# Filler matmuls, later loads and one pair's transpose moved to TensorE in a fused attention and bilinear-FFN kernel

## The chip, the cores and the metric

The kernel runs on one core of one Trainium2 chip. The metric is the device time of one execution, in microseconds: 420.25 as the median of five runs, from 419.61 to 420.96. TensorE (PE in the profile) multiplies matrices, VectorE (DVE) and ScalarE (ACT) work element by element, GpSimd (POOL) issues the loads here, and SyncE (SP) issues DMA transposes.

## The reference

```python
# q, k, v: (8, 8, 576, 64) float32; bias_table: (32, 8)
scores = scale * np.matmul(q, k.transpose(0, 1, 3, 2))
bias = bias_table[bucket]                    # bucket from |i - j|
scores = scores + bias.transpose(2, 0, 1)[None, :, :, :]
attn = softmax(scores)                       # written out with max, exp and sum
attn_out = np.matmul(attn, v)
# x: (4608, 512), the heads of a token side by side
a = x @ w_a                                  # (512, 1536)
b = x @ w_b
out = (a * b) @ w_out                        # (1536, 512)
```

There are 8 batches with 8 heads of 576 tokens. The bias depends on the distance of two tokens alone and enters as a factor after the exponential.

## The kernel before

**Tiling.** Two heads make a pair, so there are 32 pairs, four to a batch; pair p belongs to batch p // 4. Of the 576 tokens the first 512 are four tiles of 128, and the last 64 are a tail. For each pair TensorE makes the scores by key tile (`qk`, line 407, and `qk_tail`), ScalarE takes the exponential (`ex`, 429), VectorE multiplies with the bias factor (`mul`, 434; the table lies in `W_sb`, loaded by `load_w`), and TensorE multiplies with v (`av_mm`, 561 and 565, with one more column of ones that gives the sum of the weights). `av_norm` (579, 580) divides by the sum on VectorE and writes the pair's result into `XG[p % 2]`, token by token. `t_x` turns it into the layout that the FFN needs, `xn_sb`, with one tile for each of the four pairs of a batch.

**Two ways to transpose.** For pairs 4 to 30 `t_x` issues two DMA transposes from SP's queue (588 for the four main tiles, 591 for the tail). For the first four pairs and the last one it uses TensorE: `tr_x` (602) transposes tiles into a half of the PSUM tile `trb`, and `copy_x` (299 on VectorE, 297 on ScalarE) copies them into `xn_sb`. The queries and keys of batches 0 and 1 are transposed on TensorE as well, those of later batches by DMA, half a batch at a time (`t_half`, 379 and 371).

**FFN.** It runs over nine chunks of 512 tokens. A chunk has 36 units of four matmuls: `ff_in` (626) makes pa and pb from `xn_sb`, all four pairs of a batch in one sum, ScalarE copies pa (`ff_ha`, 633), VectorE multiplies (`ff_g`, 636), and `ff_o_mm` (663) multiplies with w_out; `ff_o_out` (668) copies to `ob` and ScalarE's queue stores it. Chunk c takes the main tokens of batch c; chunk 8 takes all tails.

**Order.** It is written by hand; each engine does its instructions in the order of the program text. The first pairs follow the string `opening`, whose tokens are steps: `<name` is a load on POOL's queue, `S` scores, `E` exponential, `M` product, `AV` and `N` attention matmul and its normalisation, `X` and `CX` transpose and copy of the result, `TQ`, `TK`, `TZ` and `CQ`, `CK`, `CZ` the same for queries, keys and tails, `F`, `H`, `G` parts of the FFN, and `w` a matmul of zeros into a tile `warm` that nothing reads. From pair 7 on a loop over slots s (one pair each) lays out the steps of pair s and the attention matmuls of pair s - 1, with nine FFN units in between (`U`). At the end of a slot stand the transposes and loads for later batches. `load_half(b, g)` loads half g of batch b: keys, queries, with g = 0 the tails too, and values. The b of the loop counts from 0, so b = 3 is the fourth batch.

```python
late = [A(3, 4), lambda: t_x(s - 1), U]
...
if s % 4 == 1 and 2 <= b < B:
    load_vt(b)
if s % 4 == 3:
    load_half(b + 1, 0)
if s % 4 == 1 and b > 2:
    load_half(b, 1)
```

`load_vt(b)` loads the tails of v of a batch (170) into one of two buffers; it waits until the attention matmuls of batch b - 2 have read it. POOL's loads stand in one queue, so what comes behind waits as well.

Of the kernel before, what the change touches and what calls it, by code (L numbers as in the profile page):

```python
# [13 lines left out]
def kernel(  # L14
# [11 lines left out]
    nc = tc.nc  # L26
    FP32 = mybir.dt.float32
# [4 lines left out]
    B, H, S, Dh = 8, 8, 576, 64  # L32
# [183 lines left out]
                            op=mybir.AluOpType.subtract)  # L216
    warm = ps_av.tile([128, 512], FP32, tag="av", name="warm")

    def warm_up(n):
        for _ in range(n):  # L220
            nc.tensor.matmul(out=warm[:, :], lhsT=zero_sb[:, 0:128], rhs=zero_sb[:, :],
                             start=True, stop=True)

    warm_up(5)
    nc.scalar.activation(out=eb_sb[0:NB, :], in_=bt_sb[0:NB, :], func=ACTF.Exp)
# [358 lines left out]
    def t_x(p, jqs=range(5), eng=None):  # L584
        b, hp = divmod(p, 4)
        c0 = SM * B + ST * b
        if 4 <= p < NP - 1:
            nc.sync.dma_start_transpose(
                out=xn_sb[hp][:, SM * b:SM * b + SM].rearrange("d (j c) -> d j c", j=4),
                in_=XG[p % 2][:, 0:4, :, :].rearrange("p j h d -> p (j h d)"))  # L590
            nc.sync.dma_start_transpose(
                out=xn_sb[hp][:, c0:c0 + ST],
                in_=XG[p % 2][0:ST, 4, :, :].rearrange("p h d -> p (h d)"))
            return
        tr_x(p, jqs)
        copy_x(p, jqs, eng)

    def tr_x(p, jqs):
        st[p]["tx", jqs[0]] = ps = tr_half()
# [5 lines left out]
    def copy_x(p, jqs, eng):  # L605
        b, hp = divmod(p, 4)
        c0 = SM * B + ST * b
        ps = st[p]["tx", jqs[0]]
        q0, q1 = 128 * jqs[0], min(SM, 128 * jqs[-1] + 128)
        copy(eng, xn_sb[hp][:, SM * b + q0:SM * b + q1], ps[:, 0:q1 - q0])  # L610
        if jqs[-1] == 4:
            copy(eng, xn_sb[hp][:, c0:c0 + ST], ps[:, SM - q0:S - q0])
# [98 lines left out]
    def v_next(s):  # L711
# [8 lines left out]

    opening = """
        <k0 <q0 <q123h0 <tk <k23 <k1 <W0 <v0 <vtb <Wtb <W1 <W3 <vta <W2 <tq <R1 <q123h1 <v1 <R0 <Wta
        <wa0 <wb0 TK0 PD0 CK0:A PD1 w TQ0 PU1 CQ00:D CQ01:D w S000 PU0 TQ20 E000 PC1 TQ10 S001 CQ20:D
        CQ10:D TQ30 E001 PC0 TZ1 CQ30:D S011 CZ1:A PC2 <vt1b <uq <vt1a <R2 <wa1 <q4 <R3 <k4 <wb1 <vb1b
        <q5 <k5 <uk <vb1a <wb2 <q6 <q7 <k6 <k7 <wa2 <wo S010 PF0 TK3 PF1 E011 TK2 CK3:D CK2:D E010 w
        S300 M001 TK1 E300 M000 KS CK1:D EK w S101 V0:D E101 w S100 E100 M101 w S200 AV00 M300 E200 S301
        N00 TZ0 E301 M100 X00 S201 CX00:D AV10 E201 M200 N10 CZ0:A M201 X10 TQ11 M301 CX10:A T0 CQ11:A
        V1:D TQ31 ET0 S111 M010 AV20 E111 MT0 T1 N20 AV30 CQ31:A ET1 M011 TQ21 LH S110 N30 X20 CQ21:A
        S310 CX20:A MT1 X30 E110 AV01 CX30:D M111 FA0a E310 M110 S210 FB0a N01 HA0a S211 E210 FA1a G0a
        AV11 HA1a M210 E211 X01 T2 N11 TZ0x CX01:A T3 ET2 FB1a M211 X11 FA2a G1a CX11:A S311 MT2 HA2a  # L730
# [11 lines left out]

    def step(token):
        nonlocal nxt
        if token == "w":
            warm_up(1)
            return
        if token[0] == "<":
            load(token[1:])
            return  # L750
        name, _, e = token.partition(":")
        eng = ACT if e == "A" else nc.vector
        kind = name.rstrip("0123456789abfx")
        num = name[len(kind):]
        if kind in ("FA", "HA", "FB", "G"):
            unit = (0, int(num[:-1]), 256 if num[-1] == "b" else 0, 512 if num[-1] == "f" else 256)
            if kind in ("FA", "FB"):
                ff_in(*((wa_sb, "pa") if kind == "FA" else (wb_sb, "pb")), *unit)
                nxt += 1
            else:  # L760
                (ff_ha if kind == "HA" else ff_g)(*unit)
            return
        if kind == "FO":
            ff_o_mm(0, int(num[0]), int(num[1]))
            nxt += 1
            return
        if kind == "HO":
            ff_o_out(0, int(num))
            return
        i = [int(x) for x in num.rstrip("x")]  # L770
        p = i[0] if i else 0
        first = p < 4
        jqs = None
        if len(i) > 1 and i[1] < 2:
            jqs = ((h0, h1) if first else ((0, 1, 2), (3, 4)))[i[1]]
        second = int(num.endswith("x"))
        if kind == "TQ":
            tr_qh(p, i[1]) if len(i) > 1 else tr_q(p)
        elif kind == "CQ":
            copy_qh(p, i[1], eng) if len(i) > 1 else copy_q(p, eng)  # L780
        elif kind == "TK":
            tr_k(p)
        elif kind == "CK":
            copy_k(p, eng)
        elif kind == "TZ":
            tr_tails(second, p)
        elif kind == "CZ":
            copy_tails(second, p, eng)
        elif kind == "KS":
            tail_keys0()  # L790
        elif kind == "EK":
            ex_keys0()
        elif kind == "S":
            qk_half(p, i[1], (i[2],)) if first else qk(p, 0, (i[1],))
        elif kind == "E":
            ex_half(p, i[1], i[2]) if first else ex(p, i[1])
        elif kind == "M":
            mul_half(p, i[1], i[2]) if first else mul(p, i[1])
        elif kind == "T":
            qk_tail(p)  # L800
        elif kind == "ET":
            ex_tail(p)
        elif kind == "MT":
            mul_tail(p)
        elif kind == "V":
            b, g = divmod(p, 2)
            v_in(b, 4 * g, 4 * g + 4, eng)
        elif kind == "AV":
            av_mm(p, jqs, *((ps_ff, "ffn") if first and i[1] == 0 and p % 2 else ()))
        elif kind == "N":  # L810
            av_norm(p, jqs)
            if not first and i[1] == 1:
                t_x(p)
        elif kind == "X":
            tr_x(p, jqs)
        elif kind == "CX":
            copy_x(p, jqs, eng)
        elif kind == "PU":
            pad_z(1, p)
        elif kind == "PF":  # L820
            nc.vector.memset(tl[0][64 * p:64 * p + 64, :, :, Dh - Dh * p:128 - Dh * p], 0.0)
        elif kind == "PC":
            if p == 2:
                pad_ones(1)
            else:
                nc.vector.memset(vt[1][64 * p:64 * p + 64, :, 1 - p, :], 0.0)
        elif kind == "PD":
            pad_x(p)
        elif kind == "LH":
            load_half(2, 0)  # L830
            load_half(2, 1)
        elif kind == "LV":
            load_vt(2)
        else:
            raise ValueError(token)
# [4 lines left out]
    t_half(2, 0)  # L840

    quotas = {7: 9, 8: 9}
    for s in range(7, NP + 1):
        new = s < NP
        U = "unit"
        A = lambda *jq: (lambda: av(s - 1, jq))
        steps = []
        if new:
            steps += [lambda: (qk(s, 0), ex(s, 0))]
        if new:  # L850
            head = [U, lambda: ex(s, 1), A(0, 1, 2), U, lambda: mul(s, 0), lambda: t_q(s + 1), U,
                    lambda: mul(s, 1)]
            late = [A(3, 4), lambda: t_x(s - 1), U]
            if shared(s):
                pair = [lambda: v_next(s), lambda: (qk(s, 2), ex(s, 2), ex_rows(s)), U,
                        lambda: ex(s, 3), U, lambda: mul(s, 2), lambda: mul_rows(s)]
            else:
                pair = [lambda: v_next(s), lambda: (qk(s, 2), ex(s, 2)), U, lambda: ex(s, 3),
                        lambda: t_k(s + 1, ACT), U, lambda: mul(s, 2)]
            tail = [lambda: (qk_tail(s), ex_tail(s)), U, U, lambda: mul_tail(s)]  # L860
            if s % 4 == 0:
                steps += head + late + [U] + pair + [lambda: mul(s, 3)] + tail
            else:
                steps += head + pair + late + [U, lambda: mul(s, 3)] + tail
        else:
            ff["late"] = True
            steps += [A(0, 1, 2), U, U, U, A(3, 4), lambda: t_x(s - 1, (0, 1, 2)), U, U, U,
                      lambda: t_x(s - 1, (3, 4)), U, U, U]
        b = s // 4 + 1
        if s % 4 == 2 and b < B:  # L870
            t_half(b, 0)
        if s % 4 == 0 and 2 <= b - 1 < B:
            t_half(b - 1, 1)
        if s % 4 == 1 and 2 <= b < B:
            load_vt(b)
        if s % 4 == 3:
            load_half(b + 1, 0)
        if s % 4 == 1 and b > 2:
            load_half(b, 1)
        quota = quotas.get(s, 9)  # L880
        seen, put = 0, 0
        nu = sum(1 for x in steps if x is U)
        for x in steps:
            if x is U:
                seen += 1
                n = (quota * seen + nu - 1) // nu - put
                put_units(n)
                put += n
            else:
                x()  # L890
# [31 lines left out]
```

## Time and profile before

| | us |
|---|---|
| median of five runs | 420.25 (419.61 to 420.96) |
| the profiled execution | 420.24 |
| its span | 418.5 |
| TensorE matmul busy | 405.6 |
| ScalarE busy | 250.5 |
| VectorE busy | 237.3 |
| GpSimd busy | 134.0 |
| granted TensorE clock | 1.00 |

The span is from the first to the last recorded instruction of one execution; the run's time has some more around it. Rows of the timeline give the start, the length of the group, the engine and line, the operation with output and inputs, the count, and in brackets how long the engine had stood still and what ended that. Rows of the waits give the sum, the count and the longest. Matmul rows overlap: the time from start to start is shorter than the length of one.

### The profile page before, as it was taken

The numbers are of one execution on the slowest core, as the hardware profiler recorded it, in microseconds if no ns is written. First come the engines' busy times: TensorE is split into PE (matmuls) and PEld (weight loads), VectorE is DVE, ScalarE is ACT, GpSimd is POOL, SyncE is SP. The second block draws the span as 40 slices with busy tenths as digits, with TensorE's granted clock in tenths as the row PEclk, the third lists the DMA queues.
The fourth block names the chain that finished last, engine by engine and source line by source line (L and its number), as shares of the span: only waits on it lengthen the run. The fifth ranks groups of instructions, "written<-read, shape, count | busy, mean of one in ns | idle before, by whom it ended". The sixth has DMA issues, their size and how long they took to land.

```text
span 418.5 us, 9152 instructions
## 1 busy us (share of the span) xinstructions
PE 405.6 (97%) x3643; PEld 212.0 (51%) x3643; DVE 237.3 (57%) x566; ACT 250.5 (60%) x388; POOL 134.0 (32%) x191
## 2 busy tenths in 40 slices
PE   8879999989999999999999999999999999999996
PEld 3457674535555544555555555455545555444443
DVE  5778987446654776467645675476547661330430
ACT  3978885466766765667657673866567742322321
POOL 6947629669108700690049201600000000000000
PEclk9999999999999999999999999999999999999999
DMA  8999999999939980999179905940420012002004
GB/s 102 168 195 187 204 148 144 146 210 130 125 59 163 135 101 20 164 149 116 22 136 156 137 16 117 145 91 17 91 89 16 16 39 77 1 2 101 2 0 100
DMA packets 136427, 42.22 MB, mean 101 GB/s; under 512 B 114328, under 2 KB 131608, under 8 KB 136384
## 3 DMA queue, kind: packets, MB, share of 16 engines
q0 software_dynamic: 81712, 20.27, 56.2%
q1 hardware_dynamic: 49232, 12.02, 20.1%
q10 hardware_dynamic: 5440, 9.34, 7.2%
q8 instruction: 28, 0.46, 0.5%
q14 instruction: 15, 0.12, 0.1%
HBM read 39.18 MB, written 9.45 MB: 116 GB/s over the span
## 4 chain that ended last, share of the span: by engine, by line
PE 77%; DMA 13%; POOL 6%; issue 1%; ACTq 0%; SPq 0%; ACT 0%; DVE 0%; POOLq 0%
PE pb L626 20%; PE pa L626 20%; PE po L663 19%; PE av L565 7%; PE qk L407 6%; DMA wo<-in_moe_w_out_dram 4%; DMA wb<-in_moe_w_b_dram 3%; DMA kn<-in_k_dram 2%; DMA xn<-XG 2%; DMA vn<-in_v_dram 2%; PE av L561 2%; PE qkt L478 1%; POOL W L236 1%; DMA bias_tab<-tab_sb 1%; POOL qn L132 1%
## 5 line engine op out<-in xcount | busy, mean ns | idle before, releaser
L429 ACT ACTIVATE at<-qk 128x1024 bf16<-128x1024 f32 x112 | 113.4, 1029 | 28.6 <-PE qk L407 10.7
L636 DVE TENSOR_TENSOR g<-pb,ha 128x512 bf16<-128x512 f32 (+1 forms) x116 | 76.0, 655 | 75.4 <-PE pb L626 58.7
L626 PE MATMUL pa<-xn,wa 128*128 128x512 bf16 (+1 forms) x464 | 112.7, 365 | 1.3 <-DMA xn<-XG 1.3
L626 PE MATMUL pb<-xn,wb 128*128 128x512 bf16 (+1 forms) x464 | 112.5, 365 | 0.6 <-DMA wb<-in_moe_w_b_dram 0.6
L633 ACT ACTIVATE ha<-pa 128x512 f32<-128x512 f32 (+1 forms) x116 | 66.6, 574 | 66.1 <-PE pa L626 66.0
L663 PE MATMUL po<-wo,g 128*128 128x512 bf16 x420 | 98.7, 379 | 0.0
L434 DVE TENSOR_TENSOR at<-at,W 128x1024 bf16<-128x1024 bf16 x112 | 74.9, 685 | 21.1 <-ACT at L429 21.1
L626 PEld LDWEIGHTS <-wa 128*128 128x128 bf16 x464 | 41.6, 98 | 45.5 <-issue 6.3
L626 PEld LDWEIGHTS <-wb 128*128 128x128 bf16 x464 | 40.9, 98 | 42.0 <-issue 4.7
L663 PEld LDWEIGHTS <-g 128*128 128x128 bf16 x420 | 38.3, 98 | 43.0 <-issue 2.5
L579 DVE RECIPROCAL rc<-av 128x6 f32<-128x6 f32 (+3 forms) x96 | 16.3, 170 | 52.4 <-PE av L565 52.2
L668 ACT ACTIVATE ob<-po 128x512 f32<-128x512 f32 x35 | 21.0, 600 | 40.0 <-PE po L663 31.9
L565 PE MATMUL av<-vm,at 128*128 128x65 bf16 x896 | 41.2, 194 | 0.0
L170 POOL DMA_DIRECT2D vt<-in_v_dram x12 | 7.9, 670 | 103.1 <-PE av L565 99.8
L565 PEld LDWEIGHTS <-at 128*128 128x128 bf16 x896 | 37.2, 98 | 6.2
L132 POOL DMA_DIRECT2D qn<-in_q_dram x48 | 36.4, 808 | 12.0 <-DMA wo<-in_moe_w_out_dram 7.9
L580 DVE TENSOR_TENSOR XG<-av,rc 128x384 bf16<-128x384 f32 (+3 forms) x96 | 36.2, 377 | 3.3
L141 POOL DMA_DIRECT2D kn<-in_k_dram x48 | 36.2, 794 | 2.8 <-PE trb L362 1.4
L561 PE MATMUL av<-vt,att 128*128 128x130 bf16 x152 | 33.3, 219 | 0.0
L407 PE MATMUL qk<-QB,KB 64*128 64x512 bf16 x192 | 29.2, 381 | 0.4 <-ACT at L429 0.3
L508 ACT ACTIVATE att<-qkt 128x576 bf16<-128x576 f32 x24 | 15.5, 648 | 13.1 <-PE qkt L480 13.1
L561 PEld LDWEIGHTS <-att 128*128 128x128 bf16 x152 | 15.0, 98 | 7.7 <-issue 1.6
(102 smaller groups left out, 314.7 us busy)
## 6 DMA issues: line engine op xcount, KB each, us to landing
out_dram<-ob ACTq DMA_DIRECT2D x32, 256.0 KB, 2.8
vn<-in_v_dram POOLq DMA_DIRECT2D x16, 256.0 KB, 6.5
kn<-in_k_dram POOLq DMA_DIRECT2D x48, 64.0 KB, 5.1
qn<-in_q_dram POOLq DMA_DIRECT2D x48, 64.0 KB, 4.5
wa<-in_moe_w_a_dram POOLq DMA_DIRECT2D x3, 512.0 KB, 9.3
wb<-in_moe_w_b_dram POOLq DMA_DIRECT2D x3, 512.0 KB, 9.6
wo<-in_moe_w_out_dram POOLq DMA_DIRECT2D x1, 1536.0 KB, 16.6
xn<-XG SPq DMA_TRANSPOSE x54, 3.3
```

The lines of the kernel that those rows point to most:

```text
L132: nc.gpsimd.dma_start(out=by_tile(qn[b % 2])[:, h0 // 4, t, :, :], in_=q[b, h0:h1, 128 * t:128 * t + 128, :].transpose([1, 0, 2]))
L141: nc.gpsimd.dma_start(out=by_tile(kn[b % 2])[:, h0 // 4, t, :, :], in_=k[b, h0:h1, t:SM:NM, :].transpose([1, 0, 2]))
L407: nc.tensor.matmul(out=ps[:, hh, :], lhsT=kT[r, t, :], rhs=qT[r, :, :], start=True, stop=True)
L429: nc.scalar.activation(out=at[:, :, :], in_=ps[:, :, :], func=ACTF.Exp, scale=scale)
L434: nc.vector.tensor_tensor(out=at[:, :, :], in0=at[:, :, :], in1=w[:, :, S - 1 + t:S - 1 + t - SM:-1], op=MULT)
L561: nc.tensor.matmul(out=pav[:, slot, :, :], lhsT=weights_tail(p, jq), rhs=vt[i][:, hp, :, :], start=True, stop=True)
L565: nc.tensor.matmul(out=pav[:, slot, hh, :], lhsT=weights(p, t, hh, jq), rhs=vm[i][:, 2 * hp + hh, t, :], start=False, stop=True, skip_grou ...
L580: nc.vector.tensor_tensor(out=xg[0:np_, j0:j0 + n, :, :], in0=pav[0:np_, s0:s0 + n, :, 0:Dh], in1=r.unsqueeze(3).to_broadcast([np_, n, 2, ...
L626: nc.tensor.matmul(out=ps[:, 0:n], lhsT=w[df // 4][:, mc, 128 * (df % 4):128 * (df % 4) + 128], rhs=xn_sb[mc][:, 512 * c + lo:512 * c + lo ...
L633: nc.scalar.activation(out=ha[:, 0:n], in_=ff["pa", df, lo][:, 0:n], func=ACTF.Copy)
L636: nc.vector.tensor_tensor(out=g_sb[df][:, lo:lo + n], in0=ff["pb", df, lo][:, 0:n], in1=ff["ha", df, lo][:, 0:n], op=MULT)
L663: nc.tensor.matmul(out=po[:, :], lhsT=g_sb[df][:, 128 * tt:128 * tt + 128], rhs=wo_sb[:, df, :], start=(df == 0), stop=(df == NDF - 1))
```

## The change

- Fillers: `w` now has a count, and `wa` writes to a tile of its own in the pool of the attention results. In the opening the two single `w` ahead of the scores of pair 0 become `w1` and `w4`, `w2` is added behind those scores, and `wa4` behind `AV10`. The other `w` stay at one.
- Loads: the first half of the batch with b = 3 is loaded in slot 9 instead of 7 and its second half in slot 10 instead of 9; the first half of b = 4 in slot 12 instead of 11. The later ones stay in their slots.
- Pair 7, the last pair of batch 1, is transposed by `tr_x` and `copy_x`, three query tiles and then two, in the place where the two DMA transposes were issued.

```diff
-    def warm_up(n):
+    def warm_up(n, dst=None):
         for _ in range(n):
-            nc.tensor.matmul(out=warm[:, :], lhsT=zero_sb[:, 0:128], rhs=zero_sb[:, :],
-                             start=True, stop=True)
+            nc.tensor.matmul(out=(warm if dst is None else dst)[:, :], lhsT=zero_sb[:, 0:128],
+                             rhs=zero_sb[:, :], start=True, stop=True)
...
-        if 4 <= p < NP - 1:
+        if 4 <= p < NP - 1 and p != 7:
...
+    def t_pair(p):
+        for jqs in ((0, 1, 2), (3, 4)) if p == 7 else (range(5),):
+            t_x(p, jqs)
...
-        <wa0 <wb0 TK0 PD0 CK0:A PD1 w TQ0 PU1 CQ00:D CQ01:D w S000 PU0 TQ20 E000 PC1 TQ10 S001 CQ20:D
+        <wa0 <wb0 TK0 PD0 CK0:A PD1 w1 TQ0 PU1 CQ00:D CQ01:D w4 S000 w2 PU0 TQ20 E000 PC1 TQ10 S001 CQ20:D
...
-        N00 TZ0 E301 M100 X00 S201 CX00:D AV10 E201 M200 N10 CZ0:A M201 X10 TQ11 M301 CX10:A T0 CQ11:A
+        N00 TZ0 E301 M100 X00 S201 CX00:D AV10 wa4 E201 M200 N10 CZ0:A M201 X10 TQ11 M301 CX10:A T0 CQ11:A
...
-        if token == "w":
-            warm_up(1)
+        if token[0] == "w":
+            warm_up(int(token[-1]), ps_av.tile([128, 512], FP32, tag="av", name=f"fill{nxt}")
+                    if token[1] == "a" else None)
             return
...
+    load_slot = {bb: 9 if bb == 3 else 12 if bb == 4 else 4 * bb - 5 for bb in range(3, B)}
...
-            late = [A(3, 4), lambda: t_x(s - 1), U]
+            late = [A(3, 4), lambda: t_pair(s - 1), U]
...
-        if s % 4 == 3:
-            load_half(b + 1, 0)
-        if s % 4 == 1 and b > 2:
-            load_half(b, 1)
+        for bb in range(3, B):
+            for g in range(2):
+                if s == load_slot[bb] + (2 - (bb < 5)) * g:
+                    load_half(bb, g)
```

More of the change, by code (lines that the diff above doesn't have):

```diff
@@ L722 @@
         <k0 <q0 <q123h0 <tk <k23 <k1 <W0 <v0 <vtb <Wtb <W1 <W3 <vta <W2 <tq <R1 <q123h1 <v1 <R0 <Wta
-        <wa0 <wb0 TK0 PD0 CK0:A PD1 w TQ0 PU1 CQ00:D CQ01:D w S000 PU0 TQ20 E000 PC1 TQ10 S001 CQ20:D
+        <wa0 <wb0 TK0 PD0 CK0:A PD1 w1 TQ0 PU1 CQ00:D CQ01:D w4 S000 w2 PU0 TQ20 E000 PC1 TQ10 S001 CQ20:D
         CQ10:D TQ30 E001 PC0 TZ1 CQ30:D S011 CZ1:A PC2 <vt1b <uq <vt1a <R2 <wa1 <q4 <R3 <k4 <wb1 <vb1b
-        <q5 <k5 <uk <vb1a <wb2 <q6 <q7 <k6 <k7 <wa2 <wo S010 PF0 TK3 PF1 E011 TK2 CK3:D CK2:D E010 w
-        S300 M001 TK1 E300 M000 KS CK1:D EK w S101 V0:D E101 w S100 E100 M101 w S200 AV00 M300 E200 S301
-        N00 TZ0 E301 M100 X00 S201 CX00:D AV10 E201 M200 N10 CZ0:A M201 X10 TQ11 M301 CX10:A T0 CQ11:A
+        <q5 <k5 <uk <vb1a <wb2 <q6 <q7 <k6 <k7 <wa2 <wo S010 PF0 TK3 PF1 E011 TK2 CK3:D CK2:D E010 w1
+        S300 M001 TK1 E300 M000 KS CK1:D EK w1 S101 V0:D E101 w1 S100 E100 M101 w1 S200 AV00 M300 E200 S301
+        N00 TZ0 E301 M100 X00 S201 CX00:D AV10 wa4 E201 M200 N10 CZ0:A M201 X10 TQ11 M301 CX10:A T0 CQ11:A
         V1:D TQ31 ET0 S111 M010 AV20 E111 MT0 T1 N20 AV30 CQ31:A ET1 M011 TQ21 LH S110 N30 X20 CQ21:A
```

## The prediction

> **What bounds the kernel now.** I read the page first: the busy row by slices, and the DMA row under it. Each slice is 10.46 us.
>
> ```profile
> PE   8879999989999999999999999999999999999996
> DMA  8999999999939980999179905940420012002004
> ```
>
> TensorE is full from the fourth slice on except for one 8, the slice from 83.7 to 94.2 us. The loss that a change can recover is in the first three slices and in that one. DMA is full up to 115 us. Next the waits of TensorE, then the chain that ended last, in order of time.
>
> ```profile
> PE trb L602 <- DVE XG L580: 1.6, 3, 0.9
> PE pa L626 <- DMA xn<-XG: 1.3, 1, 1.3
> PE pb L626 <- DMA wb<-in_moe_w_b_dram: 0.6, 1, 0.6
> ```
> ```profile
> 72.47 8.44 DMA kn<-in_k_dram
> 80.91 1.32 SPq L379
> 82.33 7.94 DMA xn<-XG
> ```
>
> The chain goes through loads until 90.3 us and through TensorE afterwards. The single wait at L626 (second and third columns: once, 1.3 us) is where the two meet: pair 7, the last pair of batch 1, reaches xn by a DMA transpose that is issued at 82.33, behind a transpose of q at L379, and lands 7.94 us later (the median of the 54 such transposes is 3.3). So I read the timeline around it.
>
> ```profile
> 80.72 1.89 PE L663 MATMUL po<-wo,g 128*128 128x512 bf16 x8
> ...
> 85.26 0.60 ACT L668 ACTIVATE ob<-po 128x512 f32<-128x512 f32 x1 [0.72 <-DMA out_dram<-ob]
> ...
> 87.35 0.93 PE L407 MATMUL qk<-QB,KB 64*128 64x512 bf16 x4 [0.25 <-ACT at L429]
> ...
> 88.22 0.82 PE L626 MATMUL pa<-xn,wa 128*128 128x512 bf16 x3
> ...
> 90.31 0.38 PE L626 MATMUL pa<-xn,wa 128*128 128x512 bf16 x1 [1.28 <-DMA xn<-XG]
> ```
>
> Three of the four pa matmuls start from 88.22; the fourth needs pair 7. At 0.216 us from start to start it would be issued at 88.87, and it comes at 90.31: **1.44 us lost**. No later TensorE wait is longer than 0.3 us, so what is won here reaches the end.
>
> **Pair 7 on TensorE.** Two SP transposes go. In come five PE transposes, three DVE copies, and one wait. In slot 8 the five stand directly behind the attention matmuls of query tiles 3 and 4, ahead of the po unit at 80.72. The first three read XG that was ready at 79.35 (L580, 78.79 plus 0.56). The last two need the normalisation whose last step on DVE (L580, 81.52, 0.28 long) ends at 81.80. In the changed program they also wait for DVE's copy of the first three, because both halves of `trb` share one bank. The copy follows on DVE where the copy of v started (81.72); 128x384 takes 0.338 us on the one such row, so it ends at 82.06. Add 0.06 for the hand-over (XG ended at 18.92, its transpose started at 18.98) and two transposes at 0.056: the po unit starts at about 82.24. **Delay: 1.52 us.** DVE's three copies add about 0.75 us to an engine that is busy 3.6 of the 10 us from 80 to 90, and the copy of v behind them has no reader before slot 9.
>
> [...]
>
> ```profile
> 32.49 0.33 PE L602 MATMUL trb<-ident,XG 128*128 128x128 bf16 x3
> 32.66 0.39 PE L485 MATMUL qkt<-ZB,KT 128*128 128x128 bf16 x4
> ```
>
> Three transposes hold the engine for 0.17 us, 0.056 each. [...]
>
> **What of the 1.52 is absorbed.** Before, TensorE's po units ended at 86.93 and pa began at 88.22: 1.29 us for four qk matmuls, because their banks waited for ScalarE. ScalarE was itself held 0.72 us at 85.26 by an output transfer. In the new order the po unit that feeds this ob ends at about 85.8 and the exponentials of the rows at 86.05 (84.55 plus 1.5), so ob runs from 86.05, 0.79 later and not 1.5. The exponential at 86.27 moves to 87.06 and ends at 88.08; that of the tail (87.19, 0.65 long) ends at 88.63. The po units end at 88.45, the first qk pair goes at once, the second at 88.69, pa at about 88.95. Pair 7 has been in xn since about 82.7, so four pa matmuls end at 88.95 + 0.87 = 89.82, where the next attention matmul started at 90.53. **Gain: 0.71 us.** The products for that attention step are ready by about 89.1 (88.02 and 88.19 before, plus 0.79), so it can start.
>
> **Loads later.** On POOL's queue only one thing moves: the two vt loads of batch 3 (L170) now stand before the thirteen loads of its first half instead of behind. They must wait until the attention matmuls of pair 7 have read the old vt, which ends at 80.88. POOL therefore stands still from about 71.7 to 81, and everything behind, the second half and the fourth batch's first half too, starts up to 10.5 us later. Their first reader is the transpose of k and q in slot 10; before, these loads landed by about 91, now by about 102. With 8 us for a transpose as crowded as the one above, they are there by about 110, and slot 12 uses them from about 119. Cover: some 9 us. Pair 9's transpose is queued behind them on SP; its space XG is written again by pair 11 near 120 and its xn is read at 133.8 (the first pa of chunk 2), so it is covered as well. The fourth batch's own move changes no order on POOL. I cost the part at nothing; without the cover, each us of lateness beyond 9 would be a us at slot 12. The other bound is no gain either: after pair 7 has left the DMA path, TensorE waits for no load there.
>
> **The fillers.** Nine full matmuls are added: three before the first scores, two behind them, four behind AV10.
>
> ```profile
> 6.93 0.61 PE L221 MATMUL warm<-zero_sb 128*128 128x512 bf16 x1
> ...
> 14.20 0.38 PE L221 MATMUL warm<-zero_sb 128*128 128x512 bf16 x1
> ```
>
> The same filler takes 0.61 us and later 0.38: TensorE runs at half rate to about 13.7, although the page's granted clock reads 9 in every slice. At 0.427 us from start to start (five in 2.32), three push the first scores (L445) from 7.52 to about 8.64, two push TQ20 on by another 0.85. [...] The rows say who was waited for.
>
> ```profile
> 11.58 2.85 ACT L451 ACTIVATE ath<-qkh 128x1024 bf16<-128x1024 f32 x3
> ...
> 24.69 0.69 DVE L460 TENSOR_TENSOR ath<-ath,W 128x1024 bf16<-128x1024 bf16 x1 [2.04 <-DMA W<-bias_tab]
> ```
>
> From 10.79 to 18.17 ScalarE has no gap, so a faster TensorE gains nothing there. The fillers make its first exponential start at 9.3 instead of 8.17, the next at about 11 to 11.3 instead of 9.2, and the stretch at 11.58 start 1.2 to 1.5 later. By 21.36 TensorE is some 0.7 to 1.1 late (the vt wait of 0.67 at 17.46 is used up). The four fillers behind AV10 take 0.86 at full rate and end before the copy that TensorE waits for there. Then everything meets VectorE's wait of 2.04 for the bias load, which no engine moves, the waits of 0.88 and 0.54 for XG at 26.5 and 27.65, and the 0.59 for wb at 30.23. Cost: 0; if that cover fails, up to 2.0, the lateness of the second exponential.
>
> **Sum.** Profiled time 420.24, of which 418.5 span and 1.74 around it. Span 418.5 - 0.71 = 417.79, time 419.53. The median of the runs shown is 420.25, 0.01 above that execution: **419.6**.
>
> **Rivals.** (1) *More is absorbed.* If the copy comes sooner, or ScalarE runs ahead because no batch-3 load slows the output transfers (the 0.72 wait at 85.26), the delay costs nothing and all of 1.44 stays: 418.8. Against it: the five transposes themselves and the DVE chain are real. (2) *The wait only changes its name.* TensorE waits for DVE as long as it waited for the DMA: 1.52 against 1.44, absorbed nothing, 420.3. For it: three waits of just this kind (1.6 us) stand in the opening. (3) *Slower.* The fillers before and behind the first scores cost what ScalarE's chain is late, and VectorE's bias wait does not take it up: 420.25 - 0.71 + 2.0 = 421.5. It decides once the lateness left at 30.2 us passes 1.55 (0.71 plus 0.84). For it: ScalarE is saturated behind the fillers and cannot catch up before 18.17. Against it: the 2.04 at 24.69.
>
> **Numbers.** My sum 0.50 (own range 419.2 to 420.0), more absorbed 0.20, renamed wait 0.14, slower 0.16. A measurement of this kernel can tell about 0.2%, 0.84 us: faster is below 419.41, slower above 421.09. Of my sum a third falls below 419.41 (0.17), with nearly all of (1) that is 0.36 faster; slower is (3) less a little plus a late load, 0.15; the rest, 0.49, is the same. The range 418.7 to 420.9 takes in (1), (2) and the page's transpose price and leaves out most of (3).
>
> **What would show it.** Right: no DMA wait at pa near 89; instead one TensorE wait of about 1.1 us at the transposes near 82, on DVE; the vt loads on POOL near 81 with nothing for 9 us before; full-rate fillers before 14 us; and the same start of pb at 30.2. Wrong: pb later than 30.5 (the fillers cost), a wait at the qk of slot 12 (the loads are late), or a span that shrinks by over 1.2 (the opening gave something).

## The result and the profile after

The changed kernel takes 419.11 us as the median of 44 runs (417.48 to 422.43), the kernel before 420.40 over 79 runs (417.27 to 424.19). The ratio is 0.9967, with a 95% interval from 0.9955 to 0.998: **1.4 us faster** (420.4 x 0.0033), between 0.8 and 1.9. The prediction said 419.6 with a range from 418.7 to 420.9, and it held. Its sum was a gain of 0.7, though. Only 0.58 us of the measured 1.4 are found where the sum puts the gain; the rest came from nothing in the sum, so the time was met partly by luck. One of the three parts does more by itself than the whole change.

The profiled execution took 418.53 us, span 416.8, granted clock 0.998. First two of TensorE's waits, with the sum, the count and the longest, then the piece of the chain that ended last to which the first of them belongs.

```profile
PE qk L407 <- DMA QB<-qn: 1.3, 1, 1.3
...
PE trb L606 <- DVE xn L299: 1.1, 1, 1.1
```
```profile
65.69 8.92 DMA QB<-qn
```

The wait of pa for xn is gone. A wait of 1.1 us for the copy of pair 7 is there, as the sum had it. New is a wait of 1.3 us for the transposed queries of batch 2, whose transpose was issued at 65.69 and landed 8.92 us later. The timeline around slot 8, and under it the two rows of the kernel before that bound the same stretch:

```profile
74.75 0.61 PE L407 MATMUL qk<-QB,KB 64*128 64x512 bf16 x4 [1.34 <-DMA QB<-qn]
...
77.11 1.89 PE L667 MATMUL po<-wo,g 128*128 128x512 bf16 x8
...
80.86 0.27 PE L606 MATMUL trb<-ident,XG 128*128 128x128 bf16 x2 [1.07 <-DVE xn L299]
...
80.97 1.89 PE L667 MATMUL po<-wo,g 128*128 128x512 bf16 x8
...
87.82 1.04 PE L630 MATMUL pa<-xn,wa 128*128 128x512 bf16 x4
...
88.70 0.22 PE L561 MATMUL av<-vt,att 128*128 128x130 bf16 x1
```
```profile
76.00 0.61 PE L407 MATMUL qk<-QB,KB 64*128 64x512 bf16 x4
...
90.53 0.22 PE L561 MATMUL av<-vt,att 128*128 128x130 bf16 x1
```

From the po units at 77.11 to those behind the transposes it takes 3.86 us; before, from 78.36 to 80.72, it took 2.36. The stall is 1.50 us, against 1.52 in the sum. From the first scores of pair 8 to the attention matmul behind pa it takes 13.95 us (74.75 to 88.70), where it took 14.53 (76.00 to 90.53): the stretch is 0.58 shorter, against 0.71 in the sum. On POOL the two vt loads stand where they were expected, with an idle stretch of 11.64 us ahead:

```profile
79.67 1.23 POOL L170 DMA_DIRECT2D vt<-in_v_dram  x2 [11.64 <-PE av L565]
```

This stretch of TensorE, called **the stage** below, is the measure for all runs. Behind it little changes: every profile with the later loads needs between 327.9 and 328.1 us to the end of its span, and the kernel before 328.0. What lies ahead of it varies with the execution. In the opening the first pb starts at 27.57, not at 30.23. Of these 2.66 us, 1.25 lie ahead of every load of the bias table: POOL's first one starts at 7.24 us instead of 8.49, because the store of the table, issued at 4.28 in both, landed earlier, and no added instruction stands ahead of that store. The other 1.41 arise on the way from there to pb, which takes between 20.3 and 21.7 us in the profiles without the nine fillers but with the six old ones, and between 20.3 and 22.0 in those with the nine. So the change is not shown to be their cause. At the first scores of pair 8 the lead is down to 1.25, after the wait for QB.

The clock differs between the two executions too, and again not through the change. The first filler of the string, which both kernels have, is at full rate in the changed kernel:

```profile
5.23 0.39 PE L221 MATMUL warm<-zero_sb 128*128 128x512 bf16 x1
```

In the profile of the kernel before, the same filler took 0.61 us at 5.27, and one at 12.07 still did. Here the full rate stands ahead of the first added filler (5.90).

### The profile page after: what moved, and what is told of

Its sections match the earlier page's. It is cut to its first block, busy times and chain, and to the rows that moved or that the text cites. A ratio compares the mean times of both kernels' runs of the same rounds, so it can differ in the third digit from the quotient of the medians.

```text
span 416.8 us, 9172 instructions
## 1 busy us (share of the span) xinstructions
PE 404.7 (97%) x3657; PEld 212.0 (51%) x3657; DVE 237.7 (57%) x569; ACT 250.1 (60%) x388; POOL 134.3 (32%) x191
## 4 chain that ended last, share of the span: by engine, by line
PE 81%; DMA 12%; POOL 4%; issue 1%; DVE 0%; ACTq 0%; ACT 0%; SPq 0%; POOLq 0%
PE po L667 21%; PE pb L630 20%; PE pa L630 20%; PE av L565 8%; PE qk L407 6%; DMA wo<-in_moe_w_out_dram 4%; DMA wb<-in_moe_w_b_dram 2%; DMA QB<-qn 2%; DMA vn<-in_v_dram 2%; PE av L561 2%; PE qkt L478 1%; DMA kn<-in_k_dram 1%; POOL W L236 1%; DMA bias_tab<-tab_sb 1%; PE trb L416 1%
```

## The experiments

All times are medians. All ratios are to runs of the kernel before that were taken together with the variant, with 95% intervals; they are the record's own and not always the quotient of the two medians. The median of the kernel before itself lay between 420.28 and 421.12 beside the variants, so variants are compared by their ratios; 0.001 is 0.42 us. The stage is read from one profile of each. The first four edits are parts of the change, taken from the diff above.

| kernel | time, us | ratio | stage, us |
|---|---|---|---|
| before | 420.4 | 1 | 14.53 |
| whole change | 419.11 | 0.9967 (0.9955 to 0.998) | 13.95 |
| later loads alone | 417.56 | 0.992 (0.9893 to 0.9947) | 12.45 |
| pair 7 alone | 419.83 | 0.9974 (0.9954 to 0.9993) | 13.95 |
| pair 7 and later loads | 419.35 | 0.9955 (0.9934 to 0.9976) | 13.95 |
| fillers alone | 419.68 | 0.9974 (0.9951 to 0.9998) | 15.56 |
| later loads and fillers | 417.75 | 0.9907 (0.9871 to 0.9943) | 15.27 (of an execution of 423.3 us) |
| pair 7 and fillers | 419.02 | 0.996 (0.9936 to 0.9984) | 13.94 |
| change, transposes spread | 418.51 | 0.9955 (0.9933 to 0.9978) | 12.76 |
| later loads, v first | 417.55 | 0.9916 (0.9887 to 0.9945) | 12.44 |
| change, no fillers in the opening | 420.00 | 1.0004 (0.9983 to 1.0025) | 13.94 |
| later loads, no fillers in the opening | 418.02 | 0.9938 (0.992 to 0.9956) | 12.43 |
| later loads, fillers, early queries | 416.43 | 0.9882 (0.9845 to 0.9918) | 12.44 |

### The parts alone

**Later loads alone.** `t_x` and the string stay as before:

```diff
+    load_slot = {bb: 9 if bb == 3 else 12 if bb == 4 else 4 * bb - 5 for bb in range(3, B)}
...
-        if s % 4 == 3:
-            load_half(b + 1, 0)
-        if s % 4 == 1 and b > 2:
-            load_half(b, 1)
+        for bb in range(3, B):
+            for g in range(2):
+                if s == load_slot[bb] + (2 - (bb < 5)) * g:
+                    load_half(bb, g)
```

> The kernel before with the later loads alone; pair 7 stays on the DMA transpose and no filler is added. My prediction's theory (the loads are worth nothing by themselves, the gain is pair 7's): the wait of 1.3 us for xn near 90 us stays and the time stays at 420.4, within 0.3 us. Rival (the crowd of batch-3 loads is what makes pair 7's transpose late): POOL stands still from about 72 to 81 us, the transpose issued near 82.3 us lands in about 3.3 us instead of 7.9, the wait for xn is gone without any work on TensorE, and the time falls by 1.4 us, to 419.0.

Measured: 417.56, ratio 0.992, 3.4 us below the kernel before (2.2 to 4.5 by the interval, which lies wholly below that of the whole change). The rival was right, and more so than it said. First POOL and the transposes of q and pair 7 on SP's queue, in the kernel before and then with the later loads; then TensorE:

```profile
71.53 3.29 POOL L141 DMA_DIRECT2D kn<-in_k_dram  x4
...
77.48 4.75 SPq L379 DMA_TRANSPOSE QB<-qn  x1
```
```profile
81.27 1.37 POOL L170 DMA_DIRECT2D vt<-in_v_dram  x2 [11.51 <-PE av L565]
...
76.59 1.34 SPq L379 DMA_TRANSPOSE QB<-qn  x1
81.79 1.21 SPq L588 DMA_TRANSPOSE xn<-XG  x1
83.10 1.17 SPq L591 DMA_TRANSPOSE xn<-XG  x1
```
```profile
76.34 0.61 PE L407 MATMUL qk<-QB,KB 64*128 64x512 bf16 x4 [0.93 <-DMA QB<-qn]
...
87.38 0.60 PE L407 MATMUL qk<-QB,KB 64*128 64x512 bf16 x4
87.91 1.04 PE L626 MATMUL pa<-xn,wa 128*128 128x512 bf16 x4
...
88.79 0.22 PE L561 MATMUL av<-vt,att 128*128 128x130 bf16 x1
```

Before, POOL issued loads of batch 3 from 71.53 on; now it issues nothing for 11.51 us ahead of 81.27. Pair 7 still goes by DMA and is issued at the same place in the queue, but the transpose of q ahead of it holds the queue for 1.34 us instead of 4.75, the two transposes of pair 7 land in 3.8 and 4.7 us instead of 6.8 and 7.9, and all four pa matmuls run through. The second gain is at 87.38: the qk matmuls no longer wait for ScalarE. Its output copy was held 0.72 us by an output transfer before, and now there is no gap ahead of it:

```profile
84.77 0.62 ACT L668 ACTIVATE ob<-po 128x512 f32<-128x512 f32 x1
```

The stage falls from 14.53 to 12.45 (76.34 to 88.79), by 2.08: 1.44 of the wait for xn, the rest, 0.64, is the wait of the qk matmuls. The other 1.3 of the 3.4 us lie outside the stage and are not explained; the interval nearly reaches down to 2.08.

**Pair 7 alone**, with `t_pair` as in the change.

```diff
-        if 4 <= p < NP - 1:
+        if 4 <= p < NP - 1 and p != 7:
...
-            late = [A(3, 4), lambda: t_x(s - 1), U]
+            late = [A(3, 4), lambda: t_pair(s - 1), U]
```

> The kernel before with pair 7 on TensorE alone. My sum: a stall of 1.1 us at the transposes near 82 us, no wait for xn near 90 us, gain 0.7 us, time 419.7. Rival (all the measured gain of 1.4 us comes from this part): 419.0. Rival (the wait only changes its name): 420.3.

Measured: 419.83, ratio 0.9974, 1.1 us below the kernel before. The interval holds the 0.9983 of the sum and the 0.9967 of the whole change, and excludes 1. The stage is 13.95, exactly as in the whole change: once pair 7 is on TensorE, the later loads shorten this stage no further. And 13.95 is 12.45 plus the stall of 1.50: beside the later loads the move only adds its stall.

**Pair 7 and later loads**, the change without fillers.

> The changed kernel without its fillers: pair 7 on TensorE and the later loads. My theory (fillers cost and gain nothing): the same time as the whole change, 419.1, ratio 0.997. Rival (the fillers give the half that my sum lacks): gain 0.7 us only, 419.7, ratio 0.9983, and the scores of pair 8 near 76 us start where they did before.

Measured: 419.35, ratio 0.9955, stage 13.95. The interval excludes the rival's 0.9983 and holds the 0.9967 of the whole change. This run shows no gain from the nine fillers: by the ratios the change is 0.5 us slower with them, well inside the noise.

**Fillers alone.** The string and `warm_up` of the change, loads and pair 7 as before.

> The kernel before with the fillers alone. Both theories of the fillers (worth nothing, or ahead by 0.7 us at 30 us) give about 420.4 here, because the wait for xn near 90 us hangs on the loads and takes up any lead; in the second one that wait grows from 1.3 to about 2.0 us. If the fillers cost what ScalarE is late, up to 2.0 us, then the wait for xn shrinks instead and the time is up to 421.0.

Measured: 419.68, ratio 0.9974 (0.9951 to 0.9998), 1.1 us below before and not the same time. The wait for xn is 1.56 and a wait for ScalarE is 1.01, so the stage is longer than before, 15.56. The profile's own time was 419.4, with POOL's first bias load at 7.63. The first scores of pair 8 start at 74.14 instead of 76.00, and the longer stage takes back 1.03 of these 1.86 us, so the wait takes up a good part of a lead, but not all. What gave the 1.1 us in the median, one profile does not show. The clock, below, is a candidate.

### Pairs of parts, and the stall

**Later loads and fillers**, pair 7 by DMA.

> The changed kernel with pair 7 back on the DMA transpose: later loads and fillers. Theory now (the later loads alone free pair 7's transpose from the crowd, and the transpose on TensorE then only adds its stall of 1.5 us): no wait for xn near 88 us, ratio 0.992 as with the loads alone, about 1.5 us below the whole change. Rival (the loads alone were lucky, and pair 7 on TensorE is worth what my sum says): ratio 0.997 to 0.9985, a wait for xn of over 0.5 us.

Measured: 417.75, ratio 0.9907, 0.006 or some 2.5 us below the whole change; the two intervals do not meet. There is no wait for xn. The theory holds. The profile, though, is of an execution that took 423.3 us, 5.5 more than the median, and is used beyond that only for what it shows of the clock.

**Spread transposes.** The whole change, with two FFN units between the transposes of pair 7:

```diff
+            if s == 8:
+                late = [A(3, 4), lambda: t_x(7, (0, 1, 2)), U, U, lambda: t_x(7, (3, 4))]
...
-                steps += head + late + [U] + pair + [lambda: mul(s, 3)] + tail
+                steps += head + late + ([U] if s != 8 else []) + pair + [lambda: mul(s, 3)] + tail
```

> The changed kernel with two FFN units between the first three and the last two transposes of pair 7, so that VectorE's normalisation and copy lie beside TensorE's work. Theory now: the wait of 1.1 us at the second transposes goes, what remains is some 0.3 us of transposes, and the time falls by about 1.1 us against the whole change, ratio 0.994. Rival (the stall is absorbed by ScalarE anyway, as in part of my sum): 0.5 us or less, ratio 0.9955 to 0.997.

Measured: 418.51, ratio 0.9955 (0.9933 to 0.9978): the interval holds both forecasts. The profile decides.

```profile
80.68 0.33 PE L606 MATMUL trb<-ident,XG 128*128 128x128 bf16 x3
80.85 1.89 PE L667 MATMUL po<-wo,g 128*128 128x512 bf16 x8
82.58 0.28 PE L606 MATMUL trb<-ident,XG 128*128 128x128 bf16 x2
82.78 0.39 PE L407 MATMUL qk<-QB,KB 64*128 64x512 bf16 x2
```

No wait is left; the three take 0.17 us and the two 0.20 to the next matmul. The stage is 12.76, 1.19 shorter than in the change and 0.31 longer than with pair 7 on DMA. So of the 1.50, 1.19 was waiting for VectorE and some 0.3 is the transposes.

**Pair 7 and fillers.**

> The changed kernel without the later loads: pair 7 on TensorE and fillers. If the fillers gain nothing: ratio 0.9974, as pair 7 alone. If they bring 0.7 us that the wait for xn no longer takes up: 0.9958. In the profile TensorE's first pb follows POOL's first load of the bias table by 20.3 to 21.7 us in all six profiles so far, with and without fillers; it should do so here.

Measured: 419.02, ratio 0.996: it does not tell 0.9974 from 0.9958. POOL's first bias load was at 7.26 and the first pb at 27.90, 20.64 later, as expected.

### The opening and the clock

**The v loads first**, on top of the later loads alone.

```diff
-        <k0 <q0 <q123h0 <tk <k23 <k1 <W0 <v0 <vtb <Wtb
+        <k0 <q0 <q123h0 <tk <k23 <k1 <v0 <vtb <W0 <Wtb
```

> The later loads alone, and in the opening the first two loads of v stand ahead of the first load of the bias table on POOL's queue, in the 2 to 2.9 us in which POOL waits for the table. Theory (the opening up to about 30 us is set by POOL's chain of loads, which is why it moves with the landing of the table and not with the fillers): first pb about 1.4 us after fewer microseconds from the table's landing, 19 to 20 us behind the first bias load instead of 20.3 to 21.7; of it the wait for the transposed q of batch 2 near 76 us takes up some, so the time is 0 to 1.4 us below the loads alone, ratio 0.989 to 0.992. Rival (the opening is set by ScalarE and VectorE): no change of either, ratio 0.992, or slower where the bias table's first part comes later.

Measured: 417.55, ratio 0.9916, the same as the later loads alone; the first pb came 20.3 us behind the first bias load, not 19 to 20. A miss: the time gains nothing. Whether POOL's chain sets the opening is not settled by it, since TensorE was at half rate for most of 14 to 18 us in that profile (a granted clock of 0.64, then 0.50) and had no wait for wb.

The granted clock differs between the runs. Its mean over a kernel's runs, and the share of the runs under 0.993 (in the profile of the kernel before the row reads 1.00 up to 14 us, where fillers took 0.61 us, so it tells only a part):

| kernel | nine fillers | mean clock | under 0.993 |
|---|---|---|---|
| before (65 runs) | no | 0.992 | 0.60 |
| later loads alone | no | 0.994 | 0.50 |
| pair 7 alone | no | 0.994 | 0.32 |
| fillers alone | yes | 0.997 | 0.05 |
| whole change | yes | 0.998 | 0.05 |
| pair 7 and fillers | yes | 0.998 | 0.00 |

The kernels that are not in the table fit: with the nine fillers the share is at most 0.10, with the six old ones alone 0.45 and 0.54. Two windows of the later loads alone show where the clock goes; the third number from the right is the granted clock:

```profile
10.00:12.00 2.00, 2.00 (x28) 1.39 (x27) 1.33 (x7) 1.48 (x4) 2.00 (x4) 0.50 0.89 131
12.00:14.00 2.00, 1.48 (x18) 0.87 (x16) 1.91 (x5) 2.00 (x3) 2.00 (x4) 0.50 1.36 184
```

The execution that the prediction read has no such windows in this row, and was at half rate all the same until about 13.7 us (a filler of 0.61 us at 12.07, one of 0.38 at 14.20). So the fillers do hold the clock up, more often though not always: in the profile of the fillers alone the row reads 0.56 and 0.59 from 12 to 16 us.

Whether a lower clock goes with a longer time, the runs of one kernel can tell. Of the 65 runs of the kernel before, the 39 under 0.993 have a median of 421.47 and the other 26 one of 420.24, 1.2 us less. For pair 7 and later loads the difference is 1.5 us, for pair 7 alone 0.4, for the later loads alone 0.0. By estimate, from 0.60 to 0.05 of the runs at 1.2 us each, holding the clock would be worth 0.7 us to the kernel before; but runs sorted after the fact do not show that the clock is the cause.

This was asked more directly by leaving out the fillers of the string, the six old ones too.

```diff
-        <wa0 <wb0 TK0 PD0 CK0:A PD1 w1 TQ0 PU1 CQ00:D CQ01:D w4 S000 w2 PU0 TQ20 E000 PC1 TQ10 S001 CQ20:D
+        <wa0 <wb0 TK0 PD0 CK0:A PD1  TQ0 PU1 CQ00:D CQ01:D  S000  PU0 TQ20 E000 PC1 TQ10 S001 CQ20:D
...
```

The three further lines of the string lose their `w1` and `wa4` in the same way.

> The changed kernel without any filler in the opening's string: the nine added ones and the six that stood there before are left out (the seven ahead of the string stay). Theory now (fillers keep TensorE's clock from falling to half rate between 8 and 18 us, which happens in some executions and not in the one that I read): mean granted clock 0.990 or lower against 0.998 of the whole change, more than half of the runs under 0.993, and the time 0.5 us or more above the whole change, ratio 0.998 to 1.000. Rival (what is lost in the opening lies under the loads anyway, as my prediction has it): clock lower, time the same, ratio 0.9967.

Measured: 420.00, ratio 1.0004 (0.9983 to 1.0025), mean clock 0.987. It is 0.0037 above the whole change, about 1.5 us, and the two intervals just miss each other; the medians are only 0.9 us apart. So all fifteen fillers together are worth time in the changed kernel, some 0.9 to 1.5 us. Its profile stays at half rate from 8 to past 20 us: the row reads 0.50 in every two microseconds from 8 to 20 and 0.61 in the next two.

The same was asked of the later loads alone, without their six fillers.

> The later loads alone, without the six fillers of the opening's string. If the lost clock costs time: clock below 0.990 and 0.5 us or more above the later loads alone, ratio 0.993 to 0.996. If the opening lies under the loads: ratio 0.991 to 0.992 with the lower clock.

Measured: 418.02, ratio 0.9938 (0.992 to 0.9956), mean clock 0.987. That is 0.0018 above the later loads alone, and the intervals overlap: neither forecast is excluded. In this profile the half rate lasts to 26 us (the row reads 0.76 from 8 to 10 and 0.50 from there on), and the first pb comes 22.8 us after the first bias load, without a wait for wb. In the eleven profiles with all fifteen fillers or with the six old ones it was 20.3 to 22.0, but 21.1 in the change without any, so half rate in the opening does not always delay pb.

In one execution half rate came with a larger loss later on. The one of 423.3 us with later loads and fillers waited 2.88 us for QB, and then:

```profile
78.32 1.04 PE L407 MATMUL qk<-QB,KB 64*128 64x512 bf16 x4 [2.88 <-DMA QB<-qn]
79.29 1.89 PE L663 MATMUL po<-wo,g 128*128 128x512 bf16 x4
```
```profile
74.00:78.00 4.00, 1.44 (x7) 0.47 (x5) 0.60 (x2) 1.48 (x2) 0.00 (x0) 0.95 1.61 125
78.00:80.00 2.00, 1.68 (x6) 0.45 (x7) 0.00 (x0) 1.04 (x2) 0.00 (x0) 0.50 1.51 201
80.00:82.00 2.00, 2.00 (x20) 1.33 (x19) 0.00 (x0) 0.90 (x1) 0.00 (x0) 0.50 1.82 237
82.00:84.00 2.00, 2.00 (x18) 1.18 (x16) 1.11 (x3) 0.00 (x0) 0.00 (x0) 0.50 0.32 66
84.00:86.00 2.00, 2.00 (x25) 1.22 (x24) 0.85 (x2) 0.56 (x1) 0.00 (x0) 0.90 0.00 0
```

The same four qk matmuls take 1.04 us instead of 0.61, four po matmuls 1.89 instead of 1.04, until about 84.4. The row reads 1.00 from 70 to 74, 0.95 from 74 to 78 and 0.50 behind that, and the scores start at 78.32: the clock had fallen before the wait was over. The stage took 15.27 instead of 12.45: **behind the wait of 2.9 us, half rate cost 2.8 more.** It is one execution, and no run was made to show that the wait is the cause; behind waits for QB of up to 1.74 us in other profiles the same four qk matmuls took 0.61 us.

### The next bound

TensorE's first scores of pair 8 wait for QB in seven of the eight profiles of the kernels above with the later loads, and in one of the four without. Its transpose stands on SP behind pair 5's. The last kernel, later loads and fillers with pair 7 on DMA, puts it ahead:

```diff
-        E61 N40 FA4b FB4b HA4b M61 T6 ET5 G4b AV41 FA5b ET6 N41 S63 FB5b
+        E61 N40 FA4b FB4b HA4b M61 T6 ET5 G4b AV41 FA5b ET6 N41 TH S63 FB5b
...
+        elif kind == "TH":
+            t_half(2, 0)
...
     pad_tl(1)
-    t_half(2, 0)
```

> Later loads and fillers, pair 7 on the DMA transpose, and the three transposes of batch 2's first keys, queries and tails stand ahead of pair 5's transposes on SP's queue instead of behind. Theory (after the later loads the next bound is TensorE's wait for the transposed q at the first scores of pair 8, 0.9 to 2.9 us in the profiles of the later loads): q's transpose is issued 1 to 3 us sooner, that wait goes or is under 0.3 us, and the time falls to 416.5 to 417, ratio 0.990 to 0.991. Rival (the transposes wait for the loads of q and not for their place on SP): wait and time as with later loads and fillers, ratio 0.991 to 0.992.

Measured: **416.43** (6 runs, 416.1 to 417.38), ratio 0.9882 (0.9845 to 0.9918). Its median is the lowest of all, and its interval lies wholly below that of the whole change. It overlaps that of later loads and fillers, so what the step itself does rests on the profile:

```profile
61.28 1.24 SPq L379 DMA_TRANSPOSE QB<-qn  x1
```
```profile
74.34 0.61 PE L407 MATMUL qk<-QB,KB 64*128 64x512 bf16 x4
```

QB is issued at 61.28, against 65.7 to 68.4 in ten other profiles, and the scores start without a wait. So the loads of q were there in time, and the place in the queue was what held it.

## Why the prediction was right or wrong

- **Pair 7 on TensorE: right.** The stall was 1.50 us against 1.52, and what it waits for is what the sum has: VectorE's normalisation, then its copy of the first three (1.07 us by the row). Transposes cost the row's price of 0.056 us each, some 0.3 for five in the spread version; the other transpose price that the prediction's range takes in is shown by no run.
- **What is absorbed: right, a little too large.** The stage gained 0.58 against 0.71. The sum took 0.79 off the stall and the runs 0.64 (1.44 + 0.64 - 1.50 is 0.58). This is the wait of the qk matmuls for ScalarE, and the sum did not see that it is a gain of its own: the later loads remove it without any move of pair 7.
- **"I cost the part at nothing ... The other bound is no gain either": right beside pair 7's move, wrong by itself.** The stage is 13.95 with and without the later loads once pair 7 is on TensorE. Alone, the loads take 2.08 us off the stage and 3.4 off the time. The two edits remove the same wait, the loads without any work on TensorE, and pair 7's move then only adds 1.50. I priced the loads only on top of the move. The profile had said it: a transpose that lands in 7.94 us where the median is 3.3 is late because of what is issued beside it. I used that figure to price a later transpose and did not ask what becomes of this one when POOL stands still from 72 to 81. Nor was it so that "TensorE waits for no load there": a wait of 1.34 us for QB came up at the first scores of pair 8.
- **The fillers, "Cost: 0": no cost was seen, and the gain was judged from one execution.** In the changed kernel the full rate came at 5.2, ahead of the first added filler (0.39 us for one at 5.23). In the change without any filler of the string, eight transposes at 6.87 took 0.41 us, against 0.64 at 6.36 in the kernel before. So the half rate from the start to 13.7 was a matter of that execution, and its row of the granted clock, 1.00 up to 14, did not say so. Over the runs, the fillers lower the share with a low clock from 0.60 to 0.05. The fifteen together are worth some 0.9 to 1.5 us in the changed kernel. For the nine added ones the four pairs of ratios give a gain of 1.1 us (fillers alone), 0.6 (with pair 7), 0.5 (with the later loads) and -0.5 (with both), each uncertain by 1 to 2 us: only the first is clear of zero, and that barely.
- **The other 0.8 us of the measured gain stays open.** The stage gives 0.58 of the 1.4. The clock is a candidate, with the 0.7 us estimated above; against it, pair 7 and later loads without the nine fillers is as fast as the whole change. The 1.25 us of lead in the one profile are no evidence, since the landing of the table's store varies as much between executions.
- **The signs.** The wait of 1.1 us on DVE, the missing wait at pa, the vt loads near 80 with POOL idle before and fillers at full rate before 14 us were seen, and no wait at slot 12; the fillers' rate says nothing, as above. "The same start of pb at 30.2" was not seen: it came 2.66 us earlier. And the span shrank by 1.7, where over 1.2 was named as a sign that the opening gave something. It did in this execution, by 1.25 at the first scores of pair 8, and what gave it is not shown. VectorE's wait of 2.04 us for the bias load, "which no engine moves", was not there: it waited 0.34 us for them, at 29.05, and the first of them started 1.25 us earlier.
- **A slip in the sum.** 420.25 - 0.71 is 419.54, and it was put down as 419.6.

Rival (1), that all of 1.44 stays, did not occur in the stage: the stall was real. Rival (2), a wait that only changes its name, was wrong by 0.6. Rival (3) did not occur. The rival that was missing is that one edit makes another needless.

## What to carry to other kernels

When a change has several parts, price each part without the others too: two edits that remove one wait gain it once, and the dearer one may be left out. Where a transfer lands in twice its usual time (7.94 us against a median of 3.3 here), first ask what is issued beside it and could be issued later; here that cost no engine anything. And read the granted clock of several runs, and the length of like matmuls beside it, before fillers are called useless.

## What the runs showed of the hardware

- In one execution a TensorE wait of 2.88 us was followed by half rate for about 6 us (a granted clock of 0.50 from 78 to 84 us, four po matmuls in 1.89 us instead of 1.04), in a stage that took 2.8 us longer.
- The granted clock read 1.00 from 0 to 14 us in the profile of the kernel before while its matmuls ran at half rate (a filler of 0.61 us, later 0.38).
- The same filler near 5.2 us ran in 0.61 us in the profile of the kernel before and in 0.39 in that of the changed kernel, though no instruction of TensorE ahead of it differs between the two.
- The DMA transposes of one pair landed in 6.8 and 7.9 us behind batch-3 loads, and in 3.8 and 4.7 where POOL had issued none for 11.5 us.
- Five 128x128 transposes in a stream of matmuls made a stage 0.31 us longer.
- The landing of one 17 KB store of the bias table, issued at 4.28 us in the three profiles where its start was read, released POOL's next load anywhere from 7.24 to 8.51 us over the thirteen.
